# Fourteen of sixteen output tiles by block products, with accumulating DMAs for one sum and for the residual

## The chip, the cores and the metric

The kernel runs on one core of a Trainium2 chip. The metric is device time in microseconds (us). A kernel is timed in several executions; the profile is of one execution, which has a time of its own.

## The reference

x has 2048 tokens of 448 channels. The first half is a linear attention block, the second a token-mixing MLP; both are modulated by six rows made from c.

```python
h = layernorm(x) * (1 + ca) + sa
x = x + ga * linear_attention(h, wqkv, wo)
h = layernorm(x) * (1 + cb) + sb
h = layernorm(h)                                   # inside the mixer
u = gelu(einsum("bsd,sf->bdf", h, w1) + b1)        # F = 1792, over the tokens
y = einsum("bdf,fs->bds", u, w2) + b2              # back to 2048 tokens
x = x + gb * transpose(y)
```

The change concerns only the last product, u with w2, and the last line.

## The kernel before, in words

Tokens are cut into 16 tiles of 128, F into 14 blocks of 128. All products are of float32 accuracy: each operand is split into a high part (ScalarE, L76) and a low part (VectorE, L77), and a plain product is three matmuls, high by high, high by low, low by high (`acc3`, L739 to L742).

**The product with w1** (the loop at L1045) runs over four groups of f blocks and, in each, over the 16 token tiles, the accumulators of a group lying in PSUM banks. While it runs, `finish_u` leaves jobs: gelu and the factor gb on u (L847, L848), the split of u into `uw`, the sums of channel halves (L863 to L866), and their splits into `ut` (t1 to t4). Beside it, L1059 adds gb * b2 to each x tile, which L1060 then parks in a DRAM scratch (`xpark`). The last group has two f blocks; the pace there is one step of six matmuls per token tile.

**The product with w2** follows (the loop at L1072). It is made in two ways:

- *Plainly* (`load1`, `split1`, `mult1`, `out1`): a step takes one f block and one or two token tiles, 3 matmuls of 448 columns for each tile.
- *By blocks* (`load_quads`, `split7`, `mult7`, `out7`): a pair of token tiles, q, is taken together. The halves of F (even and odd blocks) and the two tiles make four quadrants of w2, a11, a12, a21, a22; the halves of the 448 channels do the same for u. Seven products of half the channels take the place of eight. Their left sides are a11, a12, a22 and the sums s1 = a21 + a22, s2 = s1 - a11, s3 = a11 - a21, s4 = a12 - s2. A product has 7 pairs of matmuls, one of 448 columns (high part of w2 with high and low of u side by side, L928) and one of 224 (low part with the high one, L929). Each quadrant is loaded in two tiles, of 4 and 3 blocks (`RS`), 256 and 192 KB.

Products 0, 2, 4 and 6 of a pair add into one bank, 3 and 5 into a second, 1 has a third; `out7` copies a bank out (ScalarE, L934) between the products that continue it. VectorE adds the copies and banks together (L938) and adds the two halves of the result to x (L939, L940, L962, L963). SP then stores the tile (L943).

Before, NS7 = 5 pairs (tiles 0 to 9) go by blocks, and tiles 10 to 15 plainly. `order` writes the order out: eight plain steps of tiles 10 and 11 (LEAD), then the 35 products with the other plain steps spread between them, then ten plain steps (TAIL). The last LAST = 3 steps of tile 15 are made by `mult_last` in column parts of 336 and 112 (CUT), so that the first part is stored while the second is computed. x tiles are fetched from the scratch when their pair begins (`fetch_x`, L1043).

In each turn of that loop the order of issue is: one job of `finish_u`, then loads for up to LOAD2 = 12 steps ahead on SP's queue (L889, L969), then the splits up to SPLIT2 = 4 steps ahead (so that step n + 3 is split in turn n), then the matmuls of step n, then its outputs. After the split of a quadrant, `split7` makes the next sum (L896). Each engine works its own instructions in this order. Loaded weights, their parts, the t parts, x and copies all lie in one pool of 76 slots of 512 floats (`slot`); a new tile waits for the last user of the slot that it gets.

Of the kernel before, what the change touches and what calls it, by code (L numbers as in the profile page):

```python
# [8 lines left out]
F32 = mybir.dt.float32  # L9
F32R = mybir.dt.float32r  # L10
AF = mybir.ActivationFunctionType
ALU = mybir.AluOpType
AX = mybir.AxisListType

P = 128
S, D, F = 2048, 448, 1792
NT = S // P
NF = F // P
# [9 lines left out]
DVE_LOW = (0, 1, 13, 14, 15)  # L28
AHEAD = 8
LAG = 5  # L30
LAST, CUT = 3, 336
MOD_AT = {11: [(4, 0)], 12: [(4, 1)], 13: [(4, 2)], 14: [(4, 3)], 15: [(3, 0), (3, 1)]}
QS = {0: 2, 4: 2}
WARM = 12
# [10 lines left out]
def block_kernel(ctx: ExitStack, tc: tile.TileContext, x, wqkv, wo, w1, b1, w2, b2, c, wmod, out):  # L45
    nc = tc.nc
    xf = x.flatten_outer_dims()
    of = out.flatten_outer_dims()
# [4 lines left out]
    park = ctx.enter_context(tc.tile_pool(name="park", bufs=1, space=bass.MemoryType.DRAM))  # L53
# [8 lines left out]
    def slot(name, w=D, dt=F32, parts=P):  # L62
        return slots.tile([parts, w], dt, name=name, tag="slot", padded_shape=[P, 512])

    def tslot(name, dt=F32, parts=P, w=D):
        return tok.tile([parts, w], dt, name=name, tag="tok", padded_shape=[P, 512])
# [5 lines left out]
    def bank(name):  # L72
        return psum.tile([P, 512], F32, name=name, tag="bank")
# [26 lines left out]
    X = [None] * NT  # L100
# [435 lines left out]
    for t in range(3, NT):  # L536
# [38 lines left out]
        if t == 4:  # L575
            for g in range(4):
                w = tslot(f"wo{g}", parts=G)
# [48 lines left out]
    for ch in range(4):  # L626
        for g in range(4):
            s = slice(g * G, (g + 1) * G)
# [133 lines left out]
    for i in range(NT + LAG):  # L762
# [13 lines left out]
        t = i - LAG  # L776
# [54 lines left out]
    uparts = ctx.enter_context(tc.tile_pool(name="uparts", bufs=1, reuse_waits="tile"))  # L831
    HD = D // 2
    PAIRS, RS = NF // 2, ((0, 4), (4, 3))
    NS7 = 5
    uw, uops, ufull = {}, {}, {}

    def u_parts(r, name, src):
# [39 lines left out]


    w2v = w2.rearrange("(r e p) c -> e p r c", e=2, p=P)
    raw2, hilo, acc2, cop = {}, {}, {}, {}  # L880
    QUADS = {"a11": (0, 0), "a12": (1, 0), "a21": (0, 1), "a22": (1, 1)}

    def load_quads(q):
        for name, (fo, to) in QUADS.items():
            raw2[q, name] = []
            for r0, n in RS:
                w = slot(f"{name}_{q}_{r0}", n * P)
                c0 = (2 * q + to) * P
                nc.sync.dma_start(w.rearrange("p (r c) -> p r c", c=P), w2v[fo, :, r0:r0 + n, c0:c0 + P])  # L889
                raw2[q, name].append(w)  # L890

    def sub(q, out, a, b, op=ALU.subtract, into=None):
        res = []
        for i, (r0, n) in enumerate(RS):
            w = raw2[q, into][i] if into else slot(f"{out}_{q}_{r0}", n * P)
            nc.vector.tensor_tensor(w, raw2[q, a][i], raw2[q, b][i], op=op)  # L896
            res.append(w)
        raw2[q, out] = res


    PRODS = (("a11", "b11", 0, ("s1", "a21", "a22", ALU.add)), ("a12", "b21", 1, ("s2", "s1", "a11")),
             ("s2", "t2", 0, ("s3", "a11", "a21", ALU.subtract, "a21")),
             ("s1", "t1", 2, ("s4", "a12", "s2", ALU.subtract, "a12")), ("s3", "t3", 0, None),
             ("s4", "b22", 2, None), ("a22", "t4", 0, None))

    def split7(q, m):
        a, _, _, add = PRODS[m]
        hilo[q, m] = []
        for w, (r0, nr) in zip(raw2[q, a], RS):
            h, l = slot(f"{a}h_{q}_{r0}", nr * P, F32R), slot(f"{a}l_{q}_{r0}", nr * P, F32R)  # L910
            split(w, h, l)
            hilo[q, m].append((h, l))
        if add:
            sub(q, *add)

    def mult7(q, m):
        a, b, k, _ = PRODS[m]
        opens = m in (0, 1, 3)
        if opens:
            acc2[q, k] = bank(f"y{q}_{k}")  # L920
        ps = acc2[q, k]
        closes = m in (1, 5, 6)
        cut = hilo.pop((q, m))
        for r in range(PAIRS):
            (h, l), i = cut[r // 4], r % 4
            w, wh = uops[b, r]
            s = slice(i * P, (i + 1) * P)
            nc.tensor.matmul(ps[:, :D], h[:, s], w, start=opens and r == 0, stop=False, skip_group_check=True)  # L928
            nc.tensor.matmul(ps[:, :HD], l[:, s], wh, start=False, stop=closes and r == PAIRS - 1,  # L929
                             skip_group_check=True)  # L930

    def copy2(q, k, name):
        cop[q, name] = slot(f"c{name}_{q}")
        nc.scalar.activation(cop[q, name], acc2[q, k][:, :D], AF.Copy)  # L934

    def out2(q, k, name, t, half):
        c, x = cop.pop((q, name)), X[t][:, half * HD:(half + 1) * HD]
        nc.vector.tensor_add(c, acc2[q, k][:, :D], c)  # L938
        nc.vector.tensor_add(x, x, c[:, :HD])  # L939
        nc.vector.tensor_add(x, x, c[:, HD:])  # L940

    def store(t):
        nc.sync.dma_start(of[t * P:(t + 1) * P, :], X[t])  # L943

    def out7(q, m):
        t0, t1 = 2 * q, 2 * q + 1
        if m == 0:
            copy2(q, 0, "c1")
        elif m == 1:
            out2(q, 1, "c1", t0, 0)  # L950
        elif m == 2:
            copy2(q, 0, "c2")
        elif m == 3:
            copy2(q, 2, "c5")
        elif m == 4:
            out2(q, 0, "c5", t1, 1)
        elif m == 5:
            out2(q, 2, "c2", t0, 1)
            store(t0)
        else:  # L960
            x = X[t1][:, :HD]
            nc.vector.tensor_add(x, acc2[q, 0][:, :HD], x)  # L962
            nc.vector.tensor_add(x, acc2[q, 0][:, HD:D], x)  # L963
            store(t1)


    def load1(t, n, f):
        raw2[t, f] = slot(f"q{t}_{f}", n * P)
        nc.sync.dma_start(raw2[t, f], w2[f * P:(f + 1) * P, t * P:(t + n) * P])  # L969
# [37 lines left out]


    sevens = [(q, m) for q in range(NS7) for m in range(7)]
    plains = [(t, n, f) for t, n in ((10, 2), (12, 2), (14, 1), (15, 1)) for f in range(NF)]  # L1010
    LEAD, TAIL = 8, 10
    order = [("p", p) for p in plains[:LEAD]]
    mid = plains[LEAD:len(plains) - TAIL]
    for i, p in enumerate(sevens):
        order.append(("s", p))
        order += [("p", x) for x in mid[i * len(mid) // len(sevens):(i + 1) * len(mid) // len(sevens)]]
    order += [("p", p) for p in plains[len(plains) - TAIL:]]
    cnt = {"split": 0, "load": 0}

    def split2(n):  # L1020
# [3 lines left out]
            cnt["split"] += 1  # L1024

    def load2(n):
        while cnt["load"] < min(n, len(order)):
            kind, p = order[cnt["load"]]
            if kind == "p":
                load1(*p)  # L1030
            elif p[1] == 0:
                load_quads(p[0])
            cnt["load"] += 1

    k = NT
    jobs = [j for f in range(4) for j in finish_u(f, accs[f])]

    xleft = list(range(NT))
    xpark = [park.tile([P, D], F32, name=f"xpark{t}") for t in range(NT)]

    def fetch_x(t):
        X[t] = slot(f"xb{t}")
        nc.sync.dma_start(X[t], xpark[t])  # L1043

    k += LAG - 1  # L1045
    for o0, n in W1G[1:]:
        if early:
            accs, first = early, LAG - 1
            early = None
        else:  # L1050
            accs, first = [bank(f"up{o0 + i}") for i in range(n)], 0
        for r in range(first, NT):
            load_to(k + AHEAD)
            split_to(k + 3)
            if jobs:
                jobs.pop(0)()
            if xleft and k % 2:
                t = xleft.pop(0)
                nc.vector.scalar_tensor_tensor(X[t], mods[5], b2c[:, t:t + 1], X[t], op0=ALU.mult, op1=ALU.add)  # L1059
                nc.sync.dma_start(xpark[t], X[t])  # L1060
                X[t] = None
            step(k, accs, H2h[r], H2l[r], r == 0, r == NT - 1)
            k += 1
            if k == len(pieces) - 8:
                load2(4)
            if k == len(pieces) - 3:
                load2(LOAD2)
                split2(2)
        jobs += [j for i in range(n) for j in finish_u(o0 + i, accs[i])]


    for n, (kind, p) in enumerate(order):  # L1072
        if jobs:
            jobs.pop(0)()
        while xleft:
            t = xleft.pop(0)
            nc.vector.scalar_tensor_tensor(X[t], mods[5], b2c[:, t:t + 1], X[t], op0=ALU.mult, op1=ALU.add)
        if kind == "s":
            if p[1] == 0:
                for t in (2 * p[0], 2 * p[0] + 1):  # L1080
                    if X[t] is None:
                        fetch_x(t)
        elif p[2] == 2:
            for t in range(p[0], p[0] + p[1]):
                if X[t] is None:
                    fetch_x(t)
        load2(n + LOAD2)
        split2(n + SPLIT2)
        if n < len(order) - LAST:
            (mult7 if kind == "s" else mult1)(*p)  # L1090
            (out7 if kind == "s" else out1)(*p)
# [27 lines left out]
```

## Time and profile before

| | us |
|---|---|
| median of 3 runs | 453.87 |
| lowest and highest | 453.23, 454.25 |
| the profiled execution | 452.57 |
| its span, first to last instruction | 450.8 |
| last matmul of the w1 product begins | 319.26 |
| first block product begins | 329.06 |
| first matmul of the last, split-off steps begins | 445.46 |

The mean granted TensorE clock was 1.000. In the profile, a line like `L77 DVE TENSOR_TENSOR` names the kernel's line, the engine and the operation; names such as `s2l<-a,s2h` are output and inputs without buffer numbers. Engines are PE (TensorE), PEld (its weight loads), DVE (VectorE), ACT (ScalarE), POOL (GpSimd) and SP, which here only issues DMAs. In the order of time the first number is the start in us from the start of the span and the second the duration in us; a line with x2 merges two instructions. Groups give a count, the busy us and the mean ns. DMA rows give the queue, the count, the size of one and the median us from issue to landing. Busy shares by slice are in tenths.

### The profile page before, as it was taken

What the parts mean: (1) busy time and instruction counts of PE and PEld (TensorE: products, weight loads), DVE (VectorE), ACT (ScalarE), POOL (GpSimd) and SP (SyncE); (2) the same over time, 40 slices, a digit from 0 to 9 for tenths busy, and PEclk for the clock granted to TensorE, in tenths of its full rate; (3) what the DMA queues carried; (4) which work ended last, traced back from release to release, by engine and by line L of the source; (5) the groups of instructions that cost most, each with busy time, mean ns of one, the idle gap of its engine ahead of it and who ended that gap; (6) DMA issues with size and microseconds to landing.
All of it is one profiled execution on the core that took longest, in us unless ns stands there. A gap on an engine that the chain in (4) does not pass through costs nothing.

```text
span 450.8 us, 7295 instructions
## 1 busy us (share of the span) xinstructions
PE 446.0 (99%) x2385; PEld 411.0 (91%) x2385; DVE 356.0 (79%) x774; ACT 250.1 (55%) x559; POOL 89.0 (20%) x162
## 2 busy tenths in 40 slices
PE   9999999999999999999999999999999999999997
PEld 8689999989899999999999999999999999999997
DVE  5797787888899899896469677539696978798993
ACT  2659877755656576767675345236546262536350
POOL 2124675620014345554300000000000000000000
PEclk9999999999999999999999999999999999999999
DMA  8949899985200003222407463417960674628313
GB/s 216 308 113 205 148 188 248 223 203 163 72 0 2 23 25 104 62 49 48 138 28 242 135 203 100 132 36 233 279 184 24 197 224 125 168 100 254 111 58 100
DMA packets 60551, 61.64 MB, mean 137 GB/s; under 512 B 9376, under 2 KB 53856, under 8 KB 60512
## 3 DMA queue, kind: packets, MB, share of 16 engines
q1 hardware_dynamic: 54896, 52.45, 39.1%
q0 software_dynamic: 5616, 8.72, 11.8%
q8 instruction: 19, 0.31, 0.3%
q14 instruction: 20, 0.16, 0.1%
HBM read 45.09 MB, written 7.34 MB: 116 GB/s over the span
## 4 chain that ended last, share of the span: by engine, by line
PE 92%; POOL 3%; issue 3%; DVE 1%; ACT 0%; POOLq 0%; DVEq 0%
PE y L928 11%; PE up L742 10%; PE up L741 10%; PE up L740 10%; PE op L689 9%; PE qp L333 7%; PE y L929 6%; PE kp L333 4%; PE cacc L420 4%; PE yp L740 4%; PE yp L742 4%; PE yp L741 4%; PE warm L141 2%; PE tq L673 2%; POOL rs L289 1%
## 5 line engine op out<-in xcount | busy, mean ns | idle before, releaser
L742 PE MATMUL up<-h2h,pl 128*128 128x448 f32 x224 | 81.4, 363 | 0.0
L741 PE MATMUL up<-h2l,ph 128*128 128x448 f32 x224 | 81.2, 363 | 0.0
L740 PE MATMUL up<-h2h,ph 128*128 128x448 f32 x224 | 80.8, 361 | 0.0
L77 DVE TENSOR_TENSOR pl<-pr,ph 128x512 fp32r<-128x512 f32 (+1 forms) x60 | 36.2, 614 | 11.1 <-ACT ph L76 7.8
L741 PEld LDWEIGHTS up<-h2l,ph 128*128 128x128 f32 x224 | 42.1, 188 | 3.1
L740 PEld LDWEIGHTS up<-h2h,ph 128*128 128x128 f32 x224 | 41.9, 187 | 3.0
L742 PEld LDWEIGHTS up<-h2h,pl 128*128 128x128 f32 x224 | 42.0, 188 | 2.4
L76 ACT ACTIVATE ph<-pr 128x512 fp32r<-128x512 f32 (+1 forms) x60 | 32.7, 569 | 12.9 <-PE up L741 11.1
L934 ACT ACTIVATE cc<-y 128x448 f32<-128x448 f32 x15 | 8.2, 545 | 56.1 <-PE y L929 47.9
L740 PE MATMUL yp<-uw,qw 128*128 128x448 f32 x81 | 29.8, 367 | 0.0
L742 PE MATMUL yp<-uw,qw 128*128 128x448 f32 x81 | 29.4, 363 | 0.0
L741 PE MATMUL yp<-uw,qw 128*128 128x448 f32 x81 | 29.4, 363 | 0.0
L689 PE MATMUL op<-wph,pth 112*128 112x448 f32 x64 | 24.5, 383 | 0.0
L420 PE MATMUL cacc<-pkh,xh 128*128 128x448 f32 x64 | 24.3, 379 | 0.0
L76 ACT ACTIVATE qw<-q 128x256 fp32r<-128x256 f32 (+1 forms) x56 | 18.9, 353 | 8.0 <-DMA q<-in_B_w_dram 7.5
L689 PE MATMUL op<-wpl,pth 112*128 112x448 f32 x64 | 23.2, 363 | 0.0
L689 PE MATMUL op<-wph,ptl 112*128 112x448 f32 x64 | 23.2, 362 | 0.0
L420 PE MATMUL cacc<-pkl,xh 128*128 128x448 f32 x64 | 23.2, 362 | 0.0
L333 PE MATMUL kp<-wh,hl 128*128 128x448 f32 x60 | 21.6, 365 | 0.6 <-DVE hl L77 0.6
L77 DVE TENSOR_TENSOR qw<-q,qw 128x256 fp32r<-128x256 f32 (+1 forms) x56 | 18.8, 350 | 3.8 <-ACT qw L76 3.8
L333 PE MATMUL kp<-wh,hh 128*128 128x448 f32 x60 | 21.6, 366 | 0.0
L333 PE MATMUL qp<-wh,hh 128*128 128x448 f32 x60 | 21.6, 366 | 0.0
(214 smaller groups left out, 1233.2 us busy)
## 6 DMA issues: line engine op xcount, KB each, us to landing
pr<-in_B_w_dram SPq DMA_DIRECT2D x48, 256.0 KB, 3.0
a<-in_B_w_dram SPq DMA_DIRECT2D x20, 256.0 KB, 4.9
wm<-in_w_mod_dram SPq DMA_DIRECT2D x24, 196.0 KB, 4.9
a<-in_B_w_dram SPq DMA_DIRECT2D x20, 192.0 KB, 5.1
x<-in_A_x_dram SPq DMA_DIRECT2D x16, 224.0 KB, 4.5
xpark<-x SPq DMA_DIRECT2D x16, 224.0 KB, 1.9
q<-in_B_w_dram SPq DMA_DIRECT2D x28, 128.0 KB, 3.5
xb<-xpark SPq DMA_DIRECT2D x16, 224.0 KB, 3.9
```

Of the source, the lines that this page charges most:

```text
L76: nc.scalar.activation(hi, full, AF.Copy)
L77: nc.vector.tensor_sub(lo, full, hi.bitcast(F32))
L141: nc.tensor.matmul(warm[:, :P], ones, ones, start=True, stop=True)
L333: nc.tensor.matmul(o, a[:, ch * P:(ch + 1) * P], b, start=(n == 0), stop=(n == 10))
L420: nc.tensor.matmul(cacc[ch][:, :D], a[:, s], b, start=(t == 0 and i == 0), stop=(t == NT - 1 and i == len(todo) - 1))
L673: nc.tensor.transpose(tps[t][:G, g * P:(g + 1) * P], pn[:, g * G:(g + 1) * G], ident)
L689: nc.tensor.matmul(opb[t][:, :D], a[:, s], b, start=(n == 0), stop=(n == 11))
L740: nc.tensor.matmul(ps[:, :D], hi[:, sl], mh, start=first, stop=False)
L741: nc.tensor.matmul(ps[:, :D], hi[:, sl], ml, start=False, stop=False)
L742: nc.tensor.matmul(ps[:, :D], lo[:, sl], mh, start=False, stop=last)
L928: nc.tensor.matmul(ps[:, :D], h[:, s], w, start=opens and r == 0, stop=False, skip_group_check=True)
L929: nc.tensor.matmul(ps[:, :HD], l[:, s], wh, start=False, stop=closes and r == PAIRS - 1, skip_group_check=True)
```

## The change

Seven pairs (tiles 0 to 13) go by blocks instead of five, and only tiles 14 and 15 plainly. The order is eight two-tile plain steps of 14 and 15, then all 49 products in a row, then the six remaining plain steps of tile 14 and of tile 15, the last two of them in column halves of 224. The first quadrants are loaded ahead of the last four plain steps of the lead.

s1 is no longer made by VectorE: GpSimd issues two DMAs per pair that add a22 onto a21 in place. s3 is made as a22 - s2 in a11's buffer, which is the same matrix. `out2` adds the two halves of a result into a new tile (`ysum`) with one addition of 224 columns where there were two onto x; the last output is a ScalarE copy of 224 columns and one VectorE addition.

x of tiles 0 to 13 is no longer parked and fetched. With gb * b2 added it is stored into the output, and when a tile of results is complete, GpSimd issues a DMA that accumulates it onto the output in DRAM. So that a store has landed before its accumulation, VectorE writes one column of the stored tile, which waits for the store's DMA (`await_x`): at most three stores are left unwaited during the w1 product, and none when the w2 product's loop begins. Tiles 14 and 15 are parked and fetched as before.

```diff
-LAST, CUT = 3, 336
+LAST, CUT = 2, 224
...
-    NS7 = 5
+    NS7 = 7
...
+        raw2[q, "s1"] = raw2.pop((q, "a21"))
+        for w, a in zip(raw2[q, "s1"], raw2[q, "a22"]):
+            nc.gpsimd.dma_start(w, a, accum_op=ALU.add)
...
-    PRODS = (("a11", "b11", 0, ("s1", "a21", "a22", ALU.add)), ("a12", "b21", 1, ("s2", "s1", "a11")),
-             ("s2", "t2", 0, ("s3", "a11", "a21", ALU.subtract, "a21")),
+    PRODS = (("a11", "b11", 0, None), ("a12", "b21", 1, ("s2", "s1", "a11")),
+             ("s2", "t2", 0, ("s3", "a22", "s2", ALU.subtract, "a11")),
...
     def out2(q, k, name, t, half):
-        c, x = cop.pop((q, name)), X[t][:, half * HD:(half + 1) * HD]
+        c = cop.pop((q, name))
         nc.vector.tensor_add(c, acc2[q, k][:, :D], c)
-        nc.vector.tensor_add(x, x, c[:, :HD])
-        nc.vector.tensor_add(x, x, c[:, HD:])
+        nc.vector.tensor_add(yt(t)[:, half * HD:(half + 1) * HD], c[:, :HD], c[:, HD:])
+
+    def yt(t):
+        if t not in ysum:
+            ysum[t] = slot(f"yt{t}")
+        return ysum[t]
+
+    def add_to_x(t):
+        nc.gpsimd.dma_start(of[t * P:(t + 1) * P, :], ysum.pop(t), accum_op=ALU.add)
...
-            store(t0)
+            add_to_x(t0)
         else:
-            x = X[t1][:, :HD]
-            nc.vector.tensor_add(x, acc2[q, 0][:, :HD], x)
-            nc.vector.tensor_add(x, acc2[q, 0][:, HD:D], x)
-            store(t1)
+            y = yt(t1)[:, :HD]
+            nc.scalar.activation(y, acc2[q, 0][:, :HD], AF.Copy)
+            nc.vector.tensor_add(y, acc2[q, 0][:, HD:D], y)
+            add_to_x(t1)
...
-    plains = [(t, n, f) for t, n in ((10, 2), (12, 2), (14, 1), (15, 1)) for f in range(NF)]
-    LEAD, TAIL = 8, 10
...
+    LEAD = 8
+    order = [("p", (14, 2, f)) for f in range(LEAD)] + [("s", p) for p in sevens]
+    order += [("p", (t, 1, f)) for t in (14, 15) for f in range(LEAD, NF)]
+
+    loads = order[:4] + [("s", (0, 0))] + [p for p in order[4:] if p != ("s", (0, 0))]
...
+    def put_x(t):
+        if t in xpark:
+            nc.sync.dma_start(xpark[t], X[t])
+        else:
+            nc.sync.dma_start(of[t * P:(t + 1) * P, :], X[t])
+            stored.append(X[t])
+        X[t] = None
+
+    def await_x(n):
+        while len(stored) > n:
+            nc.vector.memset(stored.pop(0)[:, 0:1], 0.0)
...
-                nc.sync.dma_start(xpark[t], X[t])
-                X[t] = None
+                put_x(t)
+                await_x(3)
...
+        await_x(0)
+        if kind == "p" and p[2] == 2:
```

More of the change, by code (lines that the diff above doesn't have):

```diff
@@ L879, in block_kernel @@
     w2v = w2.rearrange("(r e p) c -> e p r c", e=2, p=P)
-    raw2, hilo, acc2, cop = {}, {}, {}, {}
+    raw2, hilo, acc2, cop, ysum = {}, {}, {}, {}, {}
     QUADS = {"a11": (0, 0), "a12": (1, 0), "a21": (0, 1), "a22": (1, 1)}
@@ L1009, in block_kernel @@
     sevens = [(q, m) for q in range(NS7) for m in range(7)]
-    plains = [(t, n, f) for t, n in ((10, 2), (12, 2), (14, 1), (15, 1)) for f in range(NF)]
-    LEAD, TAIL = 8, 10
[L1012 to L1017, printed above, removed]
+    LEAD = 8
+    order = [("p", (14, 2, f)) for f in range(LEAD)] + [("s", p) for p in sevens]
+    order += [("p", (t, 1, f)) for t in (14, 15) for f in range(LEAD, NF)]
+    loads = order[:4] + [("s", (0, 0))] + [p for p in order[4:] if p != ("s", (0, 0))]
     cnt = {"split": 0, "load": 0}
@@ L1026, in load2 @@
     def load2(n):
-        while cnt["load"] < min(n, len(order)):
-            kind, p = order[cnt["load"]]
+        while cnt["load"] < min(n, len(loads)):
+            kind, p = loads[cnt["load"]]
             if kind == "p":
@@ L1038, in block_kernel @@
     xleft = list(range(NT))
-    xpark = [park.tile([P, D], F32, name=f"xpark{t}") for t in range(NT)]
+    xpark = {t: park.tile([P, D], F32, name=f"xpark{t}") for t in range(2 * NS7, NT)}
+    stored = []
+    def put_x(t):
[8 more added lines that the diff above has]
+            nc.vector.memset(stored.pop(0)[:, 0:1], 0.0)
     def fetch_x(t):
@@ L1077, in block_kernel @@
             nc.vector.scalar_tensor_tensor(X[t], mods[5], b2c[:, t:t + 1], X[t], op0=ALU.mult, op1=ALU.add)
[L1078 to L1083, printed above, removed]
+            if t < 2 * NS7:
+                put_x(t)
+        await_x(0)
+        if kind == "p" and p[2] == 2:
             for t in range(p[0], p[0] + p[1]):
```

## The prediction

> **What bounds the kernel now.** I read first the page's busy times and its forty slices.
>
> ```profile
> PE 446.0 (99%) x2385; PEld 411.0 (91%) x2385; DVE 356.0 (79%) x774; ACT 250.1 (55%) x559; POOL 89.0 (20%) x162
> ...
> PE   9999999999999999999999999999999999999997
> ...
> DVE  5797787888899899896469677539696978798993
> ```
>
> TensorE (PE) is busy in every slice, and the waits list it with no wait after 300 us. So the end is set by what TensorE has to issue, plus a tail behind its last matmul. VectorE (DVE) is next, and in the last ten slices it is near full in places. Durations of matmuls overlap (363 ns against a spacing of 200 ns), so I price TensorE by the distance of starts, from its order of time:
>
> ```profile
> 328.86 0.36 PE L742 MATMUL yp<-uw,qw 128*128 128x448 f32 x1
> 329.06 0.36 PE L928 MATMUL y<-uw,a11h 128*128 128x448 f32 x1
> 329.26 0.27 PE L929 MATMUL y<-uw,a11l 128*128 128x224 f32 x1
> 329.37 0.38 PE L928 MATMUL y<-uw,a11h 128*128 128x448 f32 x1
> ...
> 331.27 0.38 PE L740 MATMUL yp<-uw,qw 128*128 128x448 f32 x1
> ```
>
> A block product is 7 pairs (448 and 224 columns), here 329.06 to 331.27: 2.21 us. The 48 plain matmuls of the lead run from 319.46 to 329.06: 0.200 us each. The stretch view from the first product to the first matmul of the split-off end checks it:
>
> ```profile
> 329.06:445.46 116.40, 116.40 (x687) 109.92 (x685) 97.20 (x215) 51.43 (x127) 0.00 (x0) 1.00 0.48 142
> ```
>
> The columns are TensorE, weight loads, VectorE, ScalarE, GpSimd, then clock, DMA share and GB/s. It holds 35 products and 195 plain matmuls: (116.40 - 195 x 0.200) / 35 = 2.21 us. TensorE has no gap here, and GpSimd does nothing.
>
> **TensorE, part by part.** A pair of tiles costs 7 x 2.21 = 15.5 us by products and 84 x 0.200 = 16.8 us plainly. Two pairs change over. From the first product on: before, 116.4 us and the last 18 matmuls (336 and 112 columns, 2.5 us), 118.9 us. After, 49 x 2.21 = 108.3; ten plain steps of tiles 14 and 15 at 0.60, 6.0; and 12 matmuls of 224 columns, which lie 0.10 to 0.11 apart where L929 issues them, 1.3: 115.6 us. The lead of eight two-tile steps is the same 9.6 us. **TensorE: -3.3 us.**
>
> The tail: before, the last matmul is followed by an addition of 112 columns (273 ns) and a store of 56 KB. After, by an addition of 224 columns (383 to 391 ns in L962 and L963) and a store of 112 KB, between the rows of 1.5 (56 KB) and 1.8 us (168 KB). **+0.25 us.**
>
> **Does VectorE keep up?** Products used to alternate with plain steps; now 49 stand in a row. Spacing counts again, not duration:
>
> ```profile
> 329.37 1.15 DVE L77 TENSOR_TENSOR a12l<-a,a12h 128x512 fp32r<-128x512 f32 x2
> 330.44 1.15 DVE L896 TENSOR_TENSOR s<-s,a 128x512 f32<-128x512 f32 x2
> 331.52 0.41 DVE L77 TENSOR_TENSOR qw<-q,qw 128x256 fp32r<-128x256 f32 x1
> ...
> 335.05 0.62 DVE L938 TENSOR_TENSOR cc<-y,cc 128x448 f32<-128x448 f32 x1
> 335.70 0.39 DVE L939 TENSOR_TENSOR xb<-xb,cc 128x224 f32<-128x224 f32 x1
> 336.13 0.39 DVE L940 TENSOR_TENSOR xb<-xb,cc 128x224 f32<-128x224 f32 x1
> 336.44 1.15 DVE L77 TENSOR_TENSOR s1l<-s,s1h 128x512 fp32r<-128x512 f32 x2
> ```
>
> (The last line is there for its start.) A low part or a sum of a quadrant takes 1.07 us; an output took 0.65 + 0.43 + 0.31 = 1.39 and will take 0.65 + 0.31 = 0.96 with one half addition gone. Per pair after: 7 low parts and 3 sums (the first one leaves VectorE) 10.7, three outputs 2.9, the last half 0.3: **13.9 of TensorE's 15.5 us**. ScalarE: 7 splits at about 1.0, three copies of 0.55, the new half copy 0.38: 9.1 us. Both fit on the mean.
>
> The order matters too, since a split is issued three products ahead of its use and outputs wait for TensorE in the same queue. With the end of product 4 of a pair at 0: output until 1.0, low part of the next a12 until 2.1, s2 until 3.2, output of product 5 until 4.2, low part of s2 until 5.3, s3 6.3, half output 6.7, low part of s1 7.7, s4 8.8, s3's 9.9. TensorE starts those products at 6.6 (a12), 8.8 (s2), 11.0 (s1), 13.3 (s3): about 3 us to spare each. ScalarE must also empty the shared bank before product 2 continues it, one product later: it can copy from 6.9 to 7.4, needed at 8.8. The tightest place is the first pair, where VectorE still cuts the last two u: low part of s2 at 331.5 against 333.5, bank copied at 332.5 against 333.5. Cover gone, each us of lateness costs one us.
>
> Here the load order moves: the first quadrants ahead of four plain weights. SP issues these four some 6 us later (about 316 to 318, landing 3.5 us later), and the fifth was cut at 320.9; up to 1.6 us late, inside the 2 us above, or up to 1 us of stall. I take 0.
>
> **DMAs, waits, stores.** Sixteen parkings become fourteen stores to the output and two parkings, same bytes and same queue; fourteen fetches vanish. Each new memset waits for the store of three tiles earlier. Behind it stand low parts of w1; but the stores are issued about 4.8 us apart and such stores land in 1.9 to 2.0 us. The memset costs between 60 ns (128x2) and 165 ns (128x128), 14 x 0.1 = 1.4 us in a stage where VectorE idles, hidden. The three held slots can only delay w1 loads asked for eight steps (some 10 us at the fastest pace) ahead.
>
> The new s1 is on GpSimd's queue. Rows:
>
> ```profile
> pk<-pk POOLq DMA_DIRECT2D x12, 224.0 KB, 4.6
> ...
> pl<-pr POOLq DMA_DIRECT2D x4, 256.0 KB, 4.3
> ```
>
> ```profile
> 406.62 5.41 SPq L889 DMA_DIRECT2D a<-in_B_w_dram  x8
> ```
>
> Eight quadrant loads take 5.1 to 6.4 us to issue and 4.9 to land (6.2 at most), the GpSimd issue 0.86 to 1.64, an accumulating DMA 3.0 to 6.6. Middle: 15.6 us; worst of every row: 20.8. The load is asked for at product 3 two pairs earlier, 19.9 us before my zero; VectorE wants s1 at 2.1, TensorE would stall from about 5.6. So 22 us are there, 25.5 before a stall. Additions to x stand in the same queue behind the s1 of a later pair; they only hold two slots longer.
>
> An accumulating DMA into DRAM is in no row: at least the plain store's 2.0, at most the worst SBUF one's 6.6 as far as rows go; I take 4.5, the median of its kind. The last one starts some 2 us (output, GpSimd issue) after the last product and lands near 6.5 to 8.6; TensorE still has 7.3 us, and the tail 3.1. Hidden. The Trainium skill ("DMA: Bandwidth & Descriptors", the anatomy of one DMA) says that the fixed cost is mostly the wait for the write's receipt and is worst toward HBM; by its figure of 2.0 us and bytes / 436 GB/s, an estimate of 2.5 us, this DMA would be hidden all the more. The SBUF rows (4.2 to 4.6) speak against that figure here, and for DRAM no row decides.
>
> **Sum.** -3.3 + 0.25 = -3.05 us. The profiled execution has a span of 450.8 and 452.57 us in all; it gives 447.75 and 449.5. It lies 1.3 us below the median of 453.87, so against the median: **450.8 us**. Products at 2.18 or 2.23 (as other spacings show) move it by -1.5 or +1.0, the start by up to +1.
>
> **Rivals.**
> 1. *s1 comes late* (slower). SP can run ahead only while slots are free. By my count of the code some 70 of 76 are live, so loads may start on TensorE's pace or after it, and DMA gets fuller: queue 0 cost 11.8% for 8.72 MB, 1.8 times queue 1 per MB, which gives some 11.6 us of DMA time per 15.5. From 25.5 us on, each us costs one in each of six pairs; the gain is eaten at 26.0, and 26.5 gives 450.8 + 6 = 456.8. Against it: the worst rows make 20.8. A rule of the skill works for it ("SBUF — State Buffer", the "DVE blocks DMA" trap and the port list): descriptors are written by GpSimd through a port pair shared with VectorE; it infers that tensor_tensor takes only the read side and does not stall them. Were it wrong, each of the two issues would wait for a VectorE instruction, 0.7 us. The early stage shows 0.86 to 1.64 us per issue with VectorE 80% busy. Chance 0.15.
> 2. *VectorE becomes the bound.* If full durations count (0.69 + 0.55, 0.62, 0.39) a pair takes 10 x 1.24 + 3 x 1.01 + 0.39 = 15.8, over 15.5: some 0.4 x 7 = 2.6 us, so 453.4. For it: slices of 9 already. Against it: the spacings above. Chance 0.15.
> 3. *The last addition ends the kernel.* If DRAM accumulation needs over 8.4 us; at 11, +2.6, 453.4. Chance 0.05.
> 4. *Nothing is gained*, because consecutive products pay 0.06 more each at their handover. 49 x 0.06 = 3: 453.8. Only pairs of product and plain step are in the trace. Chance 0.03.
>
> **Chances.** The forecast, 449.3 to 452.8, has 0.62. 0.2% (about what a measurement can tell) is 0.9 us. Rivals 2 to 4 are mostly within it. Faster 0.66, same 0.13, slower 0.21. The range 449.3 to 455.5 takes in the forecast and rivals 2 to 4 and leaves most of rival 1 out.
>
> **What would show it.** 49 products at 2.21 us without a gap; VectorE near 90% in that stretch; no TensorE wait on s2's or s1's parts or on the bank copies; s1 landing before VectorE asks for it; the last store ending behind the last accumulation. A VectorE wait of the sum s2 on GpSimd's DMA, or TensorE gaps once per pair, would make me wrong.

## The result and the profile after

The changed kernel takes **449.45 us** (median of 5 runs, 448.93 to 450.41) against 453.23 us for the kernel before on the same chip: a ratio of **0.9919, interval 0.9906 to 0.9933**, so 3.0 to 4.3 us less. The profiled execution has a span of 447.2 us. The page's first lines, the kernel after:

```profile
PE 442.0 (99%) x2410; PEld 407.3 (91%) x2410; DVE 358.4 (80%) x772; ACT 260.5 (58%) x564; POOL 112.7 (25%) x190
...
PE   9999999999999999999999999999999999999997
...
DVE  5797787888899899897559586639699899889873
...
POOL 2214675620014345554300000000112123113101
```

TensorE is still busy in every slice. VectorE now stands at 8 or 9 in the stretch of the products until the last pair, and GpSimd has work there. The stretch view, columns as before (TensorE, weight loads, VectorE, ScalarE, GpSimd, clock, DMA share, GB/s), first all from the first product to the split-off end, then two whole pairs:

```profile
328.40:442.66 114.26, 114.26 (x718) 108.37 (x716) 99.18 (x199) 62.14 (x134) 22.82 (x26) 1.00 0.70 145
328.40:343.90 15.50, 15.50 (x100) 14.72 (x99) 14.95 (x30) 9.46 (x19) 3.50 (x4) 1.00 0.84 195
343.90:359.40 15.50, 15.50 (x101) 14.71 (x100) 14.03 (x28) 8.74 (x18) 3.52 (x4) 1.00 0.75 162
```

TensorE has no gap, and a pair takes 15.5 us, of which VectorE is busy 14.0. The stretch holds 49 products and 30 plain matmuls: (114.26 - 30 x 0.200) / 49 = 2.209 us per product.

To tell the change from the rest, I read three marks in every profile: the first matmul of the w2 product ("front"), the first and last of the split-off end, and the span.

| profile | front | front to split-off end | split-off end | tail | front to end |
|---|---|---|---|---|---|
| before | 319.5 | 126.0 | 2.2 | 3.1 | 131.3 |
| after | 318.8 | 123.9 | 1.2 | 3.3 | 128.4 |
| s1_vector | 319.3 | 124.4 | 1.2 | 3.3 | 129.0 |
| x_vector | 318.9 | 124.3 | 1.2 | 3.6 | 129.1 |
| both_vector | 319.8 | 131.5 | 1.2 | 3.6 | 136.3 |
| pairs5 | 319.1 | 126.6 | 1.2 | 4.1 | 131.9 |
| pairs6 | 319.8 | 125.5 | 1.2 | 3.7 | 130.4 |
| before_cut | 319.4 | 126.6 | 1.2 | 3.4 | 131.2 |
| high_first | 321.9 | 123.9 | 1.2 | 3.4 | 128.4 |
| loads_in_order | 319.1 | 123.9 | 1.2 | 3.3 | 128.4 |
| ahead8 | 319.3 | 123.9 | 1.2 | 3.4 | 128.4 |
| ahead6 | 319.1 | 123.9 | 2.4 | 3.4 | 129.6 |

(All in us, rounded to 0.1; the fourth column is from the first to the last start of the split-off matmuls, the fifth from there to the end of the span, the sixth is the span less the front.) The front belongs to code that the change leaves alone but for the stores of x. It differs by up to 3.1 us between executions, so "front to end" is what a profile tells of the change: 131.3 to 128.4, **-2.9 us**. The other 0.7 of this pair of profiles lies ahead of the w2 product. The kernels begin with 44 small matmuls (L141). In the profile before, the first 26 of them start 0.21 us apart and the others 0.11; in the profile after, the first 15 do, so the next work of TensorE starts 1.2 us earlier. Some 0.5 us of that is lost again in short waits between 83 and 92 us. Neither belongs to the change.

### The profile page after: what moved, and what is told of

It reads as the page before. It is cut to its first block, busy times and chain, and to the rows that moved or that the text cites. A ratio compares the mean times of both kernels' runs of the same rounds, so it can differ in the third digit from the quotient of the medians.

```text
span 447.2 us, 7312 instructions
## 1 busy us (share of the span) xinstructions
PE 442.0 (99%) x2410; PEld 407.3 (91%) x2410; DVE 358.4 (80%) x772; ACT 260.5 (58%) x564; POOL 112.7 (25%) x190
## 3 DMA queue, kind: packets, MB, share of 16 engines
q1 hardware_dynamic: 53104, 46.02, 35.3%
q0 software_dynamic: 9648, 15.14, 21.6%
## 4 chain that ended last, share of the span: by engine, by line
PE 97%; DVE 1%; issue 1%; POOL 0%; ACT 0%; DVEq 0%; POOLq 0%
PE y L932 16%; PE up L742 10%; PE up L741 10%; PE up L740 10%; PE op L689 9%; PE y L933 8%; PE qp L333 7%; PE kp L333 7%; PE cacc L420 7%; PE warm L141 2%; PE tq L673 2%; PE tp L312 1%; PE yp L742 1%; PE yp L741 1%; PE yp L740 1%; PE kp L448 1%
## 5 line engine op out<-in xcount | busy, mean ns | idle before, releaser
L894 POOL DMA_DIRECT2D a<-a x14 | 12.4, 946 | 154.3 <-DMA q<-in_B_w_dram 95.6
L938 ACT ACTIVATE cc<-y 128x448 f32<-128x448 f32 x21 | 11.4, 544 | 19.1 <-PE y L933 19.1
L952 POOL DMA_DIRECT2D out_dram<-yt x14 | 13.0, 929 | 36.1 <-DVE yt L943 15.1
L333 PE MATMUL kp<-wh,hl 128*128 128x448 f32 x60 | 21.6, 365 | 0.2 <-DVE hl L77 0.2
L333 PE MATMUL kp<-wh,hh 128*128 128x448 f32 x60 | 21.6, 366 | 0.0
L333 PE MATMUL qp<-wh,hh 128*128 128x448 f32 x60 | 21.6, 366 | 0.0
L677 ACT ACTIVATE pth<-tq 112x512 fp32r<-112x512 f32 x16 | 9.6, 598 | 20.5 <-PE tq L673 17.7
L333 PE MATMUL qp<-wh,hl 128*128 128x448 f32 x60 | 21.4, 363 | 0.0
L848 DVE TENSOR_TENSOR u<-u,mod 128x448 f32<-128x448 f32 x14 | 8.7, 620 | 14.9 <-ACT u L847 14.8
```

The source lines that it names most:

```text
L333: nc.tensor.matmul(o, a[:, ch * P:(ch + 1) * P], b, start=(n == 0), stop=(n == 10))
L894: nc.gpsimd.dma_start(w, a, accum_op=ALU.add)
L952: nc.gpsimd.dma_start(of[t * P:(t + 1) * P, :], ysum.pop(t), accum_op=ALU.add)
```

## The experiments

All kernels compute the reference in full. "The changed kernel" is 0.9919 of the one before.

**s1 back on VectorE.**

```diff
-        raw2[q, "s1"] = raw2.pop((q, "a21"))
-        for w, a in zip(raw2[q, "s1"], raw2[q, "a22"]):
-            nc.gpsimd.dma_start(w, a, accum_op=ALU.add)
...
-    PRODS = (("a11", "b11", 0, None),
+    PRODS = (("a11", "b11", 0, ("s1", "a21", "a22", ALU.add, "a21")),
```

> The changed kernel with one part undone: VectorE makes s1 = a21 + a22 again (in a21's buffer), all else as changed. Theory (the gain is TensorE's issue time, the DMAs are only cover): VectorE needs 13.9 + 1.07 = 15.0 of TensorE's 15.5 us per pair, so TensorE still has no gaps and the time is that of the changed kernel, 3.1 to 4.0 us under the kernel before. Rival (VectorE's full durations count, 15.8 + 1.24 = 17.0 per pair): 1.5 x 7 = about 10 us above the changed kernel, so some 6 us above the kernel before.

Measured: 449.97 us, ratio 0.9942 (0.9931 to 0.9954), some 1.0 us above the changed kernel by the ratios, 0.6 by front to end. The rival is out by far. But "no gaps" was a little wrong too: in the first pair TensorE waits 0.3 us for `cc` on VectorE, ahead of a22's product.

**Additions to x back on VectorE.**

```diff
-        c = cop.pop((q, name))
+        c, x = cop.pop((q, name)), X[t][:, half * HD:(half + 1) * HD]
         nc.vector.tensor_add(c, acc2[q, k][:, :D], c)
-        nc.vector.tensor_add(yt(t)[:, half * HD:(half + 1) * HD], c[:, :HD], c[:, HD:])
+        nc.vector.tensor_add(x, x, c[:, :HD])
+        nc.vector.tensor_add(x, x, c[:, HD:])
...
-            add_to_x(t0)
+            store(t0)
```

(and tile t1 likewise; all tiles parked and fetched)

> The changed kernel with the other part undone: x of all tiles is parked and fetched, VectorE adds both halves of each output to it, and SP stores the tile. Theory (VectorE must fit under TensorE by the spacing of its instructions): 13.9 + 3 x 0.43 + 0.43 = 15.6 us per pair against 15.5, 0.1 x 7, less the 3 us that the splits are ahead: 0 to 1.5 us above the changed kernel, 2 to 3.8 us under the kernel before. Rival (the DRAM accumulation itself carries the gain, by the fetches that vanish): at the kernel before or above it.

Measured: 449.81 us, ratio 0.9945 (0.9930 to 0.9960): 1.2 us above the changed kernel by the ratios, 0.6 by front to end. As the theory says, and the rival is out: with its sixteen parkings and fetches this kernel still keeps most of the gain. The trace shows the 15.6 us itself. VectorE's last result that a22's product needs is ready 1.23, 1.11, 0.97 and 0.84 us early in the first four pairs, 0.13 less each time (15.6 against 15.47), and in the fifth and sixth nothing is left and TensorE loses 0.4 us.

**Both back on VectorE** (the two edits together).

> The changed kernel with both DMA parts undone: seven pairs, products in a row, but s1 and the additions to x on VectorE. Theory: VectorE needs 13.9 + 1.07 + 1.7 = 16.7 us per pair against TensorE's 15.5, 1.2 x 7 = 8.4 us less the 3 us of lead: 5 to 8 us above the changed kernel, 1 to 4.5 above the kernel before, with TensorE gaps in every pair. Rival (VectorE has room enough, DMAs do nothing for the time): within 1 us of the changed kernel.

Measured: 457.57 us, ratio 1.0111 (1.0093 to 1.0129), 8.7 us above the changed kernel; from front to the split-off end 131.5 instead of 123.9 us, 7.6 more. The size is the theory's, and so is the bound: a pair takes 16.67 us here, against 16.7 added up, and VectorE is busy nearly all of it (stretch view of one pair, from one start of a22's product to the next):

```profile
360.23:376.89 16.66, 15.73 (x98) 14.67 (x98) 16.42 (x34) 8.40 (x17) 0.00 (x0) 1.00 0.56 164
```

The place is another one than I had thought of. TensorE's waits in this kernel (engine, line, releaser, total us, times, longest):

```profile
PE y L928 <- DVE cc L938: 6.0, 6, 1.5
```

(A wait is listed from the end of the matmul before. Durations overlap, so by the spacing of starts the loss is some 0.16 us larger each time.) All six are ahead of a22's product, the last of a pair, and what they wait for is not a low part but the addition that reads the bank out after product 4, which product 6 continues. The order of VectorE in the same kernel:

```profile
389.67 1.15 DVE L77 TENSOR_TENSOR a22l<-a,a22h 128x512 fp32r<-128x512 f32 x2
390.75 1.15 DVE L77 TENSOR_TENSOR a11l<-a,a11h 128x512 fp32r<-128x512 f32 x2
391.82 1.15 DVE L896 TENSOR_TENSOR a<-a,a 128x512 f32<-128x512 f32 x2
392.89 0.62 DVE L938 TENSOR_TENSOR cc<-y,cc 128x448 f32<-128x448 f32 x1
```

```profile
393.56 0.47 PE L928 MATMUL y<-ut,a22h 128*128 128x448 f32 x1 [0.93 <-DVE cc L938]
```

The low part of a11 and the sum s1 of the *next* pair stand ahead of the addition in VectorE's queue, and TensorE waits 0.93 us for the bank although a22's parts have been ready for 2.7 us. In the changed kernel the same addition stands here:

```profile
354.00 1.16 DVE L77 TENSOR_TENSOR a11l<-a,a11h 128x512 fp32r<-128x512 f32 x2 [1.03 <-ACT a11h L76]
355.10 0.62 DVE L942 TENSOR_TENSOR cc<-y,cc 128x448 f32<-128x448 f32 x1
355.75 0.39 DVE L943 TENSOR_TENSOR yt<-cc 128x224 f32<-128x224 f32 x1
```

```profile
357.12 0.37 PE L932 MATMUL y<-ut,a22h 128*128 128x448 f32 x1
```

It is done by 355.75, and product 6 starts at 357.12: **1.4 us to spare**, not the 3 us of the low parts. With s1 put back ahead of it (1.07 us) the spare is 0.3. The first pair, in which VectorE is busy longest (14.95 us in the changed kernel), overdraws it: that is s1_vector's small wait.

**Five pairs, everything else changed.**

```diff
-    NS7 = 7
+    NS7 = 5
...
+    plains = [(t, n, f) for t, n in ((10, 2), (12, 2), (14, 1), (15, 1)) for f in range(NF)]
```

(and the order of the kernel before)

> Both DMA parts, the stores of x into the output and the column halves at the end as in the changed kernel, but five pairs in the order of the kernel before. Theory (only the two further pairs and the cut at the end move TensorE's issue time): 0.6 less for the cut, 0.25 more for the tail, so 0 to 0.7 us under the kernel before. Rival (taking work from VectorE is worth something by itself): 2 us or more under it.

Measured: 452.89 us, ratio 1.0010 (0.9999 to 1.0020). The DMAs alone gain nothing; the rival is out. It is some 0.5 us above the theory's upper end. The marks put that in a tail of 4.1 us instead of 3.3, and the trace says where in it: the last store lands 2.4 us after the last matmul's start in both kernels, and what follows, SP's closing waits on its semaphores and the end of the program, takes 1.7 us here and 1.0 in the changed kernel (1.3 with six pairs). Why it differs is open; it is no part of the theory.

**Six pairs.**

> As the changed kernel, but six pairs, and the plain steps of tiles 12 to 15 in the manner of the order before. Theory (each pair saves 84 x 0.200 - 7 x 2.21 = 1.33 us): 1.3 us above the changed kernel, some 1.7 to 2.4 us under the kernel before. Rival (the products in a row are what counts, or the whole gain comes with the last pair): at the kernel before, or at the changed kernel.

Measured: 452.29 us, ratio 0.9980 (0.9967 to 0.9992): 0.9 us under the kernel before, 2.8 above the changed one, off the theory by more than a microsecond in the ratio. The marks say where: front to split-off end is 126.6, 125.5 and 123.9 us with five, six and seven pairs, 1.1 and 1.6 per pair, **1.4 on the mean against 1.33 worked out**. In the profiles the rest is the tail (3.7, behind the last store, as in pairs5) and the front (319.8). So the pairs carry the gain, one after the other, and products need no row of their own for it.

**The cut of the end alone**, in the kernel before (`LAST, CUT = 2, 224`).

> The kernel before with only the end changed: two plain steps of tile 15 in column halves of 224 instead of three in 336 and 112. Theory: TensorE 0.6 us less, tail 0.25 more, so 0.35 us less, hard to tell from none. Rival (the small second part hides the first store and addition better): up to 0.5 us more.

Measured: 452.82 us, ratio 0.9990 (0.9981 to 0.9998): 0.1 to 0.9 us less. By the marks, +0.6 - 1.0 + 0.3 = -0.1. Small, as expected.

**Wide matmuls first, then narrow ones.**

```diff
+        for r in range(PAIRS):
+            (h, l), i = cut[r // 4], r % 4
+            w, wh = uops[b, r]
+            s = slice(i * P, (i + 1) * P)
             nc.tensor.matmul(ps[:, :HD], l[:, s], wh, ...)
```

> The changed kernel with another order inside a product: all seven matmuls of 448 columns, then all seven of 224, instead of pairs. In pairs a 448 takes about 0.21 and a 224 about 0.105 us; among their like they take 0.200 and 0.102 to 0.105. Theory (TensorE's issue time sets the end, and each change of width costs some 10 ns): 7 x 0.200 + 7 x 0.103 = 2.12 instead of 2.21 per product, 49 x 0.09 = 4.3 us less than the changed kernel. Rival (the spacing belongs to the weight load behind a narrow matmul, whatever its neighbours, 188 ns long): no change, or slower, since seven narrow matmuls in a row must each hide a weight load: 0.19 each, 49 x 0.6 = up to 30 us more.

Measured: 450.11 us, ratio 0.9929 (0.9916 to 0.9942), no gain; front to split-off end is the same 123.9 us. My theory here fell. TensorE in this kernel, merged:

```profile
360.21 1.61 PE L932 MATMUL y<-ut,a22h 128*128 128x448 f32 x7
361.66 0.94 PE L937 MATMUL y<-ut,a22l 128*128 128x224 f32 x7
362.43 1.60 PE L932 MATMUL y<-uw,a11h 128*128 128x448 f32 x7
```

Seven wide ones take 1.45 us (0.207 each) and seven narrow ones 0.77 (0.11 each): 2.22 us. In the changed kernel, in pairs, a wide one takes 0.21 to 0.22 and a narrow one 0.10, which adds up to the same. With fewer changes of width the wide ones are shorter and the narrow ones longer, so a price per change is not what lies behind the 2.21 us; what does, stays open. The rival allowed for no change, and that came, but not for its reason: a weight load of 188 ns is not exposed where narrow matmuls start 0.11 us apart.

**Loads in their old order.**

```diff
-    loads = order[:4] + [("s", (0, 0))] + [p for p in order[4:] if p != ("s", (0, 0))]
+    loads = order
```

> The changed kernel, but the first quadrants are loaded behind the eight plain weights of the lead, as before. Theory (s1 of the first pair landed some 3 us or more ahead of VectorE's use, and TensorE has about 2 us besides): loads come some 2 us later, no TensorE gap, time of the changed kernel within 0.4 us. Rival (the first pair is at its limit): 1 to 3 us more, as a TensorE gap ahead of the first s2 product.

Measured: 450.14 us, ratio 0.9928 (0.9914 to 0.9942), front to end 128.4 as in the changed kernel. The time is the theory's, its premise is not. In the changed kernel the second part of the first s1 was issued at 320.22, landed at 328.32, and VectorE used it at 328.98: 0.7 us ahead, not 3. Here it lands at 329.68, and VectorE waits for it:

```profile
328.63 0.69 DVE L900 TENSOR_TENSOR s<-a,a 128x512 f32<-128x512 f32 x1
329.70 0.56 DVE L900 TENSOR_TENSOR s<-a,a 128x384 f32<-128x384 f32 x1 [0.38 <-DMA a<-a]
```

TensorE does not see these 0.38 us, since the low part of s2 still comes 1.6 us before its product (1.9 in the changed kernel). So the first pair's s1 is just in time, and moving its loads buys cover but no time.

**Weights asked for later**, to price the rival of a late s1 (`LOAD2` 8 and 6 instead of 12).

> The changed kernel with weights asked for 8 steps ahead instead of 12, so the quadrants of a pair come 4 products, 8.8 us, later. This prices the rival of a late s1. By the working, 22 us were there before VectorE asks for s1 and 25.5 before TensorE stalls; now 13.2 and 16.7. Theory (issue 5.4, landing 5.7, GpSimd 0.9, accumulating DMA 3.4 to 4.3, as the changed kernel's rows have them: 15.4 to 16.3 us): VectorE waits some 2 to 3 us per pair for s1, TensorE at most little: 0 to 2 us above the changed kernel. Rival (the quadrants were slot-bound and came late anyway): no change at all.

Measured: 449.76 us, ratio 0.9931 (0.9908 to 0.9954), front to end 128.4: no change.

> The same with 6 steps ahead: the quadrants come 13.3 us later than in the changed kernel, 8.7 us are there before VectorE asks for s1 and 12.2 before TensorE stalls. Theory: 15.4 to 16.3 us of chain, so 3 to 4 us of TensorE gap in each of six pairs, 18 to 25 us above the changed kernel, as waits of VectorE's sum s2 on the accumulating DMA. Rival (the product order hides it elsewhere): under 6 us above the changed kernel.

Measured: 451.15 us, ratio 0.9951 (0.9933 to 0.9970): 1.4 us above the changed kernel, not 18 to 25. The theory's price of a late s1 fell, and the reason is in SP's order. Loads of the fourth pair, the GpSimd issue of its s1 and VectorE's use (the sum s2, `s<-a,a`), first the changed kernel, then ahead6:

```profile
346.86 5.94 SPq L889 DMA_DIRECT2D a<-in_B_w_dram  x8
...
357.18 1.77 POOL L894 DMA_DIRECT2D a<-a  x2 [9.68 <-DVE a12l L77]
...
372.60 1.16 DVE L900 TENSOR_TENSOR s<-a,a 128x512 f32<-128x512 f32 x2
```

```profile
355.25 6.58 SPq L889 DMA_DIRECT2D a<-in_B_w_dram  x8
...
365.74 0.86 POOL L894 DMA_DIRECT2D a<-a  x1 [2.51 <-DMA a<-in_B_w_dram]
367.27 0.86 POOL L894 DMA_DIRECT2D a<-a  x1 [0.66 <-ACT cc L938]
...
372.86 1.15 DVE L900 TENSOR_TENSOR s<-a,a 128x512 f32<-128x512 f32 x2
```

Loads asked for 13.3 us later were issued only 8.4 us later. In the written order these loads stand at product 3 of the second pair (TensorE gets there at 328.4 + 15.5 + 6.6 = 350.5) and, in ahead6, at product 2 of the third (some 364.0). SP ran 3.6 us ahead of TensorE in the one and 8.8 in the other. I had let it start at TensorE's pace. In both, SP waits for slots ahead of these loads (10.0 us, ended by VectorE's `s1l`, in the changed kernel; 5.2 and 5.6 us, ended by VectorE's `s3l` and by TensorE, in ahead6). With fewer weights held early, slots are free sooner; that this is the whole reason was not tried by itself. The second s1 DMA still landed 3.1 us behind its issue, 3.1 us before VectorE used its part. What ahead6 does lose lies elsewhere: the split-off end takes 2.4 us instead of 1.2, since TensorE waits there for a last split whose weights came late.

## Why the prediction was right

The forecast was 450.8 us from a median of 453.87, -3.05; the ratio gives -3.0 to -4.3, and front to end gives -2.9. By its steps:

- **TensorE, -3.3 us**: right. 49 products at 2.209 us (worked out: 2.21), no gap, the plain steps as before; pairs5, pairs6 and the changed kernel show 1.4 us per pair. Front to the last matmul fell by (126.0 + 2.2) - (123.9 + 1.2) = 3.1. The 0.2 too much is a slip in the sum: its 2.5 us for the old end includes the full duration of the last matmul (by starts it is 2.2), its 1.3 us for the new end does not.
- **Tail, +0.25**: right, 3.10 to 3.35. Half of it is the wider addition, half the larger store.
- **VectorE 13.9 of 15.5 us per pair**: 14.0 measured. ScalarE 9.1: 8.7. Rival 2 is out, by the spacing and by s1_vector and x_vector, which still win with 15.1 and 15.3 us of VectorE per pair. both_vector is where VectorE does become the bound, at 16.67 us per pair. That is the sum by spacings; by full durations it would have been 11 x 1.24 + 3 x 1.40 + 2 x 0.39 = 18.6.
- **About 3 us to spare in the order**: mis-sized. It was right for the low parts (3.2 us and more from the second pair on; for s2 in the first pair 1.9 against 2 worked out) and left out the bank that VectorE reads after product 4; there 1.4 us are spare.
- **s1**: its DMAs landed 3.3 to 8.1 us from issue (middle 4.2); three were over the 6.6 that I had as a bound, all in the first two pairs. From the third pair on, some 10 us were left instead of 6. For the fourth pair: loads from 346.86, s1 landed at 361.76, 14.9 us of chain against 15.6 worked out; VectorE used it from 372.60. A part of rival 1's condition did come: from the fourth pair on the loads wait for slots and come every 15.5 us, at TensorE's pace. But they start 3.6 us ahead of their place, and with a chain of 15 us that is far from late; ahead8 and ahead6 show that it could start later still. In the first pair, whose s1 I had not worked out at all, 0.7 us were left. That it was in time there is luck as far as the prediction goes, with TensorE's 1.9 us behind it.
- **The last addition to x**: taken as 4.5 us, measured 4.6 (3.8 to 6.0). These rows settle what the record left open:

```profile
out_dram<-yt POOLq DMA_DIRECT2D x14, 224.0 KB, 4.6
...
a<-a POOLq DMA_DIRECT2D x7, 256.0 KB, 3.4
a<-a POOLq DMA_DIRECT2D x7, 192.0 KB, 4.3
```

The last one was issued at 438.03 and landed at 442.4; the span ends at 447.2. Rival 3 is out. The estimate of 2.5 us by the Trainium skill ("DMA: Bandwidth & Descriptors", the anatomy of one DMA) is too low for an accumulating DMA; the measurement decides.

- **GpSimd's issue beside a busy VectorE**: 0.85 to 1.32 us each, with VectorE busy 14.0 of 15.5 us, nearly all of it additions or subtractions of two tiles. The Trainium skill's inference ("SBUF — State Buffer", the port list) that these do not hold up the writing of descriptors agrees with that.
- **The memsets**: 59 ns each, at the low end of the bounds, with no wait. The stores that they watch landed in 1.9 to 3.7 us, not all in 1.9 to 2.0 (in the profile before, too, up to 3.4); as they are issued some 4.8 us apart, that did no harm.
- **The fifth plain weight, up to 1.6 us late**: no TensorE wait came of it.

The measured ratio's middle, -3.7, is 0.6 beyond the sum. Within the profiles that much is in the front, which the change doesn't explain. Three kernels with the same front to end (high_first, loads_in_order, ahead8) have ratios of 0.9928 to 0.9931, 3.1 to 3.3 us less, and the interval reaches to -3.0, so nothing more needs a cause.

## What to carry to other kernels

Where TensorE has no gaps, price a change by start-to-start spacing of its instructions, and then ask only whether each other engine still fits under it; here two accumulating DMAs gained nothing themselves (pairs5), yet without both the same change loses 5 us against the kernel before (both_vector), and with either one alone it keeps most of its gain. When you look for the tightest place, go through what hands a buffer *back* (a bank read out between two products that share it) as well as what hands operands on. A load's place in the written order does not tell when it is issued: look at how far the queue really runs ahead. And work out the first round of a loop by itself: the cover that the later pairs had was not there in the first.

## What the runs showed of the hardware that I had not expected

- From start to start, an fp32r matmul of 448 columns took 0.200 us in the plain product. In the block products, a wide one took 0.21 to 0.22 and a narrow one of 224 columns 0.10 where they alternate, and 0.20 to 0.21 and 0.11 in rows of their like (high_first). A product took 2.21 us either way.
- The accumulating DMAs took about twice the DMA time of the copies: in the changed kernel queue 0, where every DMA accumulates, took 21.6% for 15.14 MB and queue 1, where none does, 35.3% for 46.02 MB, 1.43% against 0.77% per MB. GpSimd issues the ones and SP the others, and no run separates the adding from the queue. In the first five pairs the DMA engines were busy 0.75 to 0.84 of the time, and nothing on TensorE's path noticed.
